# Decode attention on one core: the V loads of 62 units move from SyncE's queue to GpSimd's own

## The chip, the core and the metric

The kernel runs on one core of one Trainium2 chip. The metric is the device time of one execution in microseconds (us); the lower the better. All inputs lie in the chip's memory (HBM), and the output is written back there.

## What is computed

Two blocks, A and B, of the same sizes and with their own inputs: single-token decode attention for 2 sequences, 32 heads of 192 dimensions, a cache of 8192 positions, all in bf16. Their outputs stand side by side.

```
q = (x @ wq)                           # x: 2 x 1 x 640, wq: 640 x 6144
scores = q . k_cache * 192**-0.5       # per head; k_cache: 2 x 32 x 8192 x 192
p = softmax(scores)
o = p . v_cache                        # v_cache: 2 x 32 x 8192 x 192
block = o @ wo                         # wo: 6144 x 640
result = concatenate([A, B], axis=-1)
```

Each number of the caches is used once, so the work is mostly a matter of reading some 837 MB.

## The kernel before

**Units.** A unit is one pair of heads of one sequence of one block; there are 64 of them (u = 0 to 63, `LASTU` = 63). A unit's K is 128 partitions of 49,152 bytes (head and position block on the partitions, 128 positions of 192 dimensions in a partition), and its V has the same shape. Each of the two is fetched by one DMA.

**Buffers.** The tile `big` holds `NBUF` = 3 buffers of that size and two small product buffers. Loads take the buffers in turn in the order of the list `loads`: K(0), K(1), V(0), K(2), V(1), K(3) and so on to K(63), V(62), V(63). Load number i may start when load i-3, which used the same buffer, has been consumed (`done`): for a K that is the fourth multiply of that unit, for a V the end of the weighted sum ("PV"). So K(u) waits for PV of unit u-3, and V(u) waits for the last multiply of K(u). The first V, V(0), waits instead for the last of the projections q, because its buffer holds the weights wq until then; K(1) waits likewise for the projections of block A.

**Work of a unit.** DVE multiplies K by q in four pieces (line 285, `dve_mul`); PE sums the products over groups of dimensions by matmuls with an identity (line 362, `pe_sum`); DVE finishes the sums (line 289) and takes the maximum over positions (line 295); GpSimd takes the maximum over partitions (line 266, `pool_ar`), and ACT makes the bias and the exponentials (lines 315 and 324). PE then forms the weighted sum over V in 64 matmuls (line 376, `pe_pv`), and it does so for unit u after the identity sums of unit u+1. DVE and ACT normalise.

**Order.** Each engine's instructions are put into a table by slot and order (`put`), sorted, and emitted as one stream (`_Stream`), with waits on counting semaphores. DVE, ACT and PE run most units in loops; SyncE (SP) and GpSimd (POOL) are written out. GpSimd's stream is some memsets at the start and then one `pool_ar` per unit.

**Transfers.** All DMAs are issued by SyncE, in one queue, in the order of `loads`: first the weights wq and x, then the K and V, then the pieces of wo, which go into buffers that have become free, and at the end the two outputs. Every DMA is issued at line 245 (`dma`). An issue waits on SyncE until its buffer is free, and what stands behind it waits too. A load adds 16 to the semaphore of its buffer (`bsem`), and its readers wait for the count that belongs to it.

**The end.** The last K and V (units 62 and 63) are followed by the pieces of wo, which take the place of K(63), V(62) and V(63) in the three buffers; PE turns the attention output, multiplies it by wo, and two small DMAs write the result.

Of the kernel before, what the change touches and what calls it, by code (L numbers as in the profile page):

```python
# [117 lines left out]
def build_kernel(nc, blocks, out):  # L118
# [16 lines left out]
    LASTU = NU - 1  # L135
    scale = float(Dh) ** -0.5
    NBUF = 3
# [9 lines left out]
    with ExitStack() as es:  # L147
        sb = lambda name, shape, dt: es.enter_context(nc.sbuf_tensor(name, shape, dt))
        ps = lambda name, shape, dt: es.enter_context(nc.psum_tensor(name, shape, dt))
        sem = lambda name: es.enter_context(nc.semaphore(name))  # L150
# [42 lines left out]
        reg = {}  # L193
        S_sp = _Stream("sp", sem("s_sp"), reg)
# [1 line left out]
        S_act = _Stream("act", sem("s_act"), reg)  # L196
        S_dve = _Stream("dve", sem("s_dve"), reg)
        S_pool = _Stream("pool", sem("s_pool"), reg)
        bsem = [sem(f"bsem{i}") for i in range(NBUF)]

        def dsem(k, n=1):
            reg[k] = (sem("d_" + "_".join(str(i) for i in k)), 16 * n)
# [6 lines left out]
        loads = [("k", 0)]  # L209
# [1 line left out]
            loads += [("k", u), ("v", u - 1)]  # L211
        loads += [("v", LASTU)]
        buf = {}
        bcount = [0] * NBUF
        for i, (kind, u) in enumerate(loads):
            buf[kind, u] = i % NBUF
            bcount[i % NBUF] += 1
            reg[(kind, u)] = (bsem[i % NBUF], 16 * bcount[i % NBUF])

        bk, b62, b63 = buf["k", LASTU], buf["v", LASTU - 1], buf["v", LASTU]  # L220
        assert (bk, b62, b63) == (2, 0, 1)
# [2 lines left out]
        for blk, rows, off, w in ((0, (WR,), woA, [("s", LASTU, NCH - 1)]), (1, (29,), wo0, [("pv", LASTU - 1)]),  # L224
                                  (1, (11, 5, 2, 1), wo1, [("pv", LASTU)])):
            r = 29 if off == wo1 else 0
            for n in rows:
                pieces.append((blk, r, r + n, off, w))
                off, r, w = off + n * D, r + n, []
# [9 lines left out]
        def back(name, u, c, n):  # L239
            i = u * NCH + c - n  # L240
            return (name, i // NCH, i % NCH) if i >= 0 else None

        def dma(out_ap, in_ap, k):
            s = reg[k][0]
            return lambda eng: eng.dma_start(out_ap, in_ap).then_inc(s, 16)
# [13 lines left out]
        def ld_kv(kind, u):  # L259
            hp, b = u // B, u % B  # L260
            blk, h = hp // PPB, 2 * (hp % PPB)
            src = blocks[blk][kind][b, h:h + 2].rearrange("s (p t) d -> (s p) t d", p=64)
            return dma(kv[buf[kind, u]], src, (kind, u))
# [154 lines left out]
        def put(eng, slot, order, fn, waits, sig, tag=None):  # L418
            t = tabs[eng].setdefault(slot, [])
            t.append((order, len(t), fn, waits, sig, tag))  # L420
# [14 lines left out]
        for u in range(NU):  # L435
            for c in range(NCH):
                w = [("k", u), ("pq", NP - 1), ("qa", NP - 1), ("qx", NP - 1), back("s", u, c, 2)]
# [32 lines left out]
        for n, p in enumerate(pieces):  # L470
            w = [("wo", n), ("ot", p[0])]
# [8 lines left out]
        def done(i):  # L480
            if i < 0:
                return None
            kind, u = loads[i]
            return ("m", u, NCH - 1) if kind == "k" else ("pv", u)
# [5 lines left out]
        for i, (kind, u) in enumerate(loads):  # L490
            w = [done(i - NBUF)]
            if i in (1, 2):
                w = [("pq", PPB * i - 1)]
            S_sp.add(ld_kv(kind, u), waits=w)
        for n in range(len(pieces)):
            S_sp.add(ld_wo(n), waits=pieces[n][4])
        for blk in range(NBLK):
# [4 lines left out]
        for n in range(1, HP + 1):  # L502
            S_pool.add((lambda n: (lambda eng: eng.memset(tri[0:n, n:n + 1], 1.0)))(n),
                       waits=[("tri0",)] if n == 1 else [], sig=("tri",) if n == HP else None)
# [5 lines left out]
        for n in range(128 // HP):  # L510
# [3 lines left out]
                  waits=[("id1",), ("place0",)], sig=("place",))  # L514
# [50 lines left out]
def bass_concat_heads__gqa_block_cached__mha_block_cached__decode_kernel(  # L565
    nc: bass.Bass,
    A_x: bass.AP,
    A_k_cache: bass.AP,
    A_v_cache: bass.AP,
    A_wq: bass.AP,  # L570
    A_wo: bass.AP,
    B_x: bass.AP,
    B_k_cache: bass.AP,
    B_v_cache: bass.AP,
    B_wq: bass.AP,
    B_wo: bass.AP,
    out: bass.AP,
):
    blocks = [
        dict(x=A_x, k=A_k_cache, v=A_v_cache, wq=A_wq, wo=A_wo),  # L580
        dict(x=B_x, k=B_k_cache, v=B_v_cache, wq=B_wq, wo=B_wo),
    ]
    build_kernel(nc, blocks, out)
# [28 lines left out]
```

## Time and profile before

| | before |
|---|---|
| median of 3 runs | 1937.1 us (1936.89 to 1937.25) |
| span of the profiled execution | 1936.0 us |
| bytes read from HBM | 836.77 MB |
| mean rate over the span | 432 GB/s |
| busy: PE, DVE, ACT, POOL | 80%, 58%, 7%, 1% |
| queue q1 (SyncE's) of the 16 DMA engines | 99.9% |

The profiled execution has no time beside its span on the page; the median of the other runs is 1.1 us above that span. Engines: PE is TensorE's matmuls, PEld its weight loads, DVE VectorE, ACT ScalarE, POOL GpSimd, SP SyncE. A line number is that of the kernel. The page's 40 slices are equal parts of the span, with the busy share in tenths; the DMA line is the mean over the 16 DMA engines. In a timeline a row begins with the start in us from the span's start and the duration in us; an arrow in brackets names what ended the engine's idle time before it. In the list of waits a row gives the engine and line that waited, what for, and the total in us, the count and the longest. In the list of DMA issues the last number is the median time from issue to landing.

### The profile page before, as it was taken

To read this page: it belongs to the slowest core of one execution; us is meant where nothing else is said; L and a number is where in the kernel's file an instruction comes from. 1 tells how busy PE (TensorE), PEld (TensorE's weight loads), DVE (VectorE), ACT (ScalarE), POOL (GpSimd) and SP (SyncE) were. 2 spreads that over 40 slices of the span, in tenths; PEclk is the share of its full clock that TensorE was granted. 3 is DMA by queue.
4 is the path that set the end of the run, shared out by engine and by line. 5 is a ranking of instruction groups with operands and counts; after the bars stand their busy time and mean duration, and the time that the engine had idled before them with its cause. 6 is when DMAs were issued, how large, how long until landed. Compare 5 with 4: busy or idle time off the path is not lost.

```text
span 1936.0 us, 19059 instructions
## 1 busy us (share of the span) xinstructions
PE 1545.0 (80%) x7728; PEld 743.0 (38%) x7729; DVE 1124.0 (58%) x907; ACT 142.3 (7%) x519; POOL 28.4 (1%) x113
## 2 busy tenths in 40 slices
PE   5777878878878878878878878878878878878878
PEld 2333434434434434434434434433433433433434
DVE  4765565565565565565565565565565565565560
ACT  3100000000000000000000000000000000000000
POOL 0000000000000000000000000000000000000000
PEclk9899989988989988989988999999999999999999
DMA  9999999999999999999999999999999999999999
GB/s 419 427 435 436 432 434 438 430 434 437 434 433 434 437 431 435 437 432 433 436 436 431 434 438 429 436 437 432 434 435 436 430 436 438 428 436 437 433 433 391
DMA packets 19610, 836.91 MB, mean 432 GB/s; under 512 B 2184, under 2 KB 2320, under 8 KB 2576
## 3 DMA queue, kind: packets, MB, share of 16 engines
q1 hardware_dynamic: 19600, 836.78, 99.9%
q8 instruction: 6, 0.10, 0.0%
q14 instruction: 4, 0.03, 0.0%
HBM read 836.77 MB, written 0.01 MB: 432 GB/s over the span
## 4 chain that ended last, share of the span: by engine, by line
DMA 49%; PE 31%; DVE 17%; issue 3%; DVEq 0%; SPq 0%; ACT 0%; ACTq 0%
DMA big<-in_B_k_cache_dram 24%; DMA big<-in_A_k_cache_dram 22%; PE ops L376 18%; DVE big L285 15%; PE scps L362 12%; DMA big<-in_B_wq_dram 2%; DVE sc L289 1%; DMA big<-in_B_wo_dram 1%; PE scps L354 0%; PE ops L368 0%; PE outps L354 0%; DVEq L285 0%; DVE qall L275 0%; PE scps L404 0%; PE oTps L390 0%
## 5 line engine op out<-in xcount | busy, mean ns | idle before, releaser
L285 DVE TENSOR_TENSOR big<-big,qall 128x6144 bf16<-128x6144 bf16 x256 | 852.7, 3351 | 490.7 <-DMA big<-in_B_k_cache_dram 260.6
L362 PE MATMUL scps<-big,ident 128*128 128x512 bf16 x3072 | 815.6, 426 | 358.2 <-DVE big L285 355.7
L376 PE MATMUL ops<-big,pb 128*34 128x384 bf16 x4096 | 676.8, 326 | 0.0
L362 PEld LDWEIGHTS scps<-big,ident 128*128 128x128 bf16 x3072 | 314.3, 107 | 852.7 <-DVE big L285 439.2
L376 PEld LDWEIGHTS ops<-big,pb 128*34 128x34 bf16 x4096 | 395.5, 98 | 258.7
L289 DVE TENSOR_REDUCE sc<-scps 128x32 f32<-128x512 f32 x256 | 175.9, 687 | 227.7 <-PE scps L362 227.7
L315 ACT ACTIVATE nb<-mg 64x1 f32<-64x1 f32 x128 | 25.8, 201 | 1707.7 <-POOL mg L266 1706.9
L324 ACT ACTIVATE pb<-sc,nb 64x128 bf16<-64x128 f32 x128 | 55.8, 436 | 7.8
L266 POOL PARTITION_ALL_REDUCE mg<-mp x64 | 25.7, 402 | 1859.1 <-DVE mp L295 1859.1
L295 DVE TENSOR_REDUCE mp<-sc 64x1 f32<-64x128 f32 x128 | 35.9, 280 | 8.3
L309 ACT ACTIVATE qall<-o_sum,rc 2x192 f32 (+1 forms) x64 | 29.0, 453 | 20.7 <-DVE o_sum L306 19.1
L306 DVE TENSOR_TENSOR o_sum<-ops,o_hi 2x192 f32<-2x192 f32 x64 | 22.1, 346 | 7.7
L354 PE MATMUL scps<-big,xw 128*128 x120 | 23.2, 351 | 2.6 <-DVE xw L271 2.2
L324 ACT ACTIVATION_READ_ACCUMULATOR pb<-sc,nb 64x1 f32 x128 | 23.7, 185 | 0.0
L303 DVE COPY o_hi<-ops 2x192 f32<-2x192 f32 x64 | 22.3, 349 | 2.0
L300 DVE RECIPROCAL rc<-ops 2x1 f32<-2x1 f32 x64 | 10.0, 156 | 21.3 <-PE ops L376 19.3
L275 DVE CAST qall<-scps 64x192 f32 x48 | 17.0, 355 | 7.2 <-PE scps L354 5.4
L280 ACT ACTIVATE qall<-scps 64x192 f32 x48 | 15.6, 324 | 30.5 <-DVE qall L275 28.2
L345 PE MATMUL oTps<-ident,xw 4*128 4x4 bf16 x5 | 0.4, 178 | 21.5 <-DMA xw<-in_B_x_dram 21.5
L354 PEld LDWEIGHTS scps<-big,xw 128*128 128x128 bf16 x120 | 12.4, 103 | 12.1 <-issue 5.9
L368 PEld LDWEIGHTS ops<-ones,rs 128*2 128x2 f32 x128 | 5.5, 82 | 26.9 <-issue 26.9
L404 PE MATMUL outps<-big,oT 128*2 128x320 bf16 x96 | 9.2, 369 | 4.6 <-DMA big<-in_A_wo_dram 4.6
(36 smaller groups left out, 67.6 us busy)
## 6 DMA issues: line engine op xcount, KB each, us to landing
big<-in_A_k_cache_dram SPq DMA_DIRECT2D x32, 6144.0 KB, 28.6
big<-in_A_v_cache_dram SPq DMA_DIRECT2D x32, 6144.0 KB, 27.6
big<-in_B_k_cache_dram SPq DMA_DIRECT2D x32, 6144.0 KB, 28.9
big<-in_B_v_cache_dram SPq DMA_DIRECT2D x32, 6144.0 KB, 27.8
big<-in_A_wq_dram SPq DMA_DIRECT2D x1, 7680.0 KB, 21.2
big<-in_B_wq_dram SPq DMA_DIRECT2D x1, 7680.0 KB, 38.2
big<-in_A_wo_dram SPq DMA_DIRECT2D x1, 7680.0 KB, 29.0
big<-in_B_wo_dram SPq DMA_DIRECT2D x1, 4640.0 KB, 29.3
```

What stands on the lines that cost most here:

```text
L266: return lambda eng: eng.partition_all_reduce(mg[u % 3][:], mp[u % 3][:], 128, bass.bass_isa.ReduceOp.max)
L285: return lambda eng: eng.tensor_tensor(prod[c % 2], t[:, c * TC:(c + 1) * TC, :], qall[:, S_dve.at(u), :].broadcast_to([128, TC, Dh]), ALU ...
L289: return lambda eng: eng.tensor_reduce(sc[u % 3][:, c * TC:(c + 1) * TC], scps[(u * NCH + c) % 3][:], AXL.X, ALU.add)
L295: ins = eng.tensor_reduce(mp[u % 3][r, s:s + 1], sc[u % 3][r, :], AXL.X, ALU.max)
L303: return lambda eng: eng.tensor_copy(o_hi[:], ops[u % 3][32:34, Dh:QW])
L306: return lambda eng: eng.tensor_tensor(o_sum[:], ops[u % 3][0:2, 0:Dh], o_hi[:], ALU.add)
L309: return lambda eng: eng.activation(qall[0:2, S_act.at(u), :], o_sum[:].unsqueeze(1), ACTF.Identity, scale=rc[u % 3][:])
L315: ins = eng.activation(nb[u % 3][r, :], mg[u % 3][r, s:s + 1], ACTF.Identity, scale=-scale)
L324: ins = eng.activation(dst, sc[u % 3][r, :].rearrange("p (g j a) -> p g a j", j=JB, a=2), ACTF.Exp, bias=nb[u % 3][r, :], scale=scale, acc ...
L354: ins = eng.matmul(qps[hp % NQ][:, 0:QW], xbc[:, blk, c, :], wq_t[blk][:, c, S_pe.at(off, QW, QW)], start=(c == 0), stop=(c == DC - 1))
L362: ins = eng.matmul(scps[(u * NCH + c) % 3][:], ident[:], prod[c % 2][:, :, j * DG:(j + 1) * DG], start=(j == 0), stop=(j == NJ - 1))
L376: ins = eng.matmul(ops[u % 3][0:MP, 0:QW], pb[u % 3][:, j0s:j0s + MP], vv[:, j, :], start=(j == 0), stop=(j == TJ - 1))
```

## The change

The loads of V for units 0 to 61 are issued by GpSimd, on a queue of its own. K, the weights, V(62) and V(63) stay on SyncE's queue. A new function `queue` tells the two apart. Since a buffer is now filled from two queues, there is a semaphore for each buffer and queue, with its own count. In GpSimd's stream the load of V(u) stands in slot u ahead of `pool_ar(u)`; it waits there, as it did on SyncE, for the last multiply of K(u). The branch for K in the last part of the diff is never taken with this `queue`.

```diff
-        bsem = [sem(f"bsem{i}") for i in range(NBUF)]
+        bsem = [[sem(f"bsem{i}_{n}") for i in range(NBUF)] for n in range(2)]
...
-        bcount = [0] * NBUF
+        bcount = [[0] * NBUF for _ in range(2)]
+
+        def queue(i):
+            kind, u = loads[i]
+            return 0 if kind == "k" or u > LASTU - 2 else 1
+
         for i, (kind, u) in enumerate(loads):
+            q = queue(i)
             buf[kind, u] = i % NBUF
-            bcount[i % NBUF] += 1
-            reg[(kind, u)] = (bsem[i % NBUF], 16 * bcount[i % NBUF])
+            bcount[q][i % NBUF] += 1
+            reg[(kind, u)] = (bsem[q][i % NBUF], 16 * bcount[q][i % NBUF])
...
             w = [done(i - NBUF)]
             if i in (1, 2):
                 w = [("pq", PPB * i - 1)]
-            S_sp.add(ld_kv(kind, u), waits=w)
+            if queue(i) == 0:
+                S_sp.add(ld_kv(kind, u), waits=w)
+            elif kind == "k":
+                put("pool", u - 2, 3, ld_kv(kind, u), w, None)
+            else:
+                put("pool", u, -1, ld_kv(kind, u), w, None)
```

## The prediction

> **What bounds the kernel now.** I read the page first: engine shares, the 40 slices, the queues, the issues.
>
> ```profile
> PE 1545.0 (80%) x7728; PEld 743.0 (38%) x7729; DVE 1124.0 (58%) x907; ACT 142.3 (7%) x519; POOL 28.4 (1%) x113
> ...
> DMA  9999999999999999999999999999999999999999
> GB/s 419 427 435 436 432 434 438 430 434 437 434 433 434 437 431 435 437 432 433 436 436 431 434 438 429 436 437 432 434 435 436 430 436 438 428 436 437 433 433 391
> ...
> q1 hardware_dynamic: 19600, 836.78, 99.9%
> ...
> big<-in_A_k_cache_dram SPq DMA_DIRECT2D x32, 6144.0 KB, 28.6
> big<-in_A_v_cache_dram SPq DMA_DIRECT2D x32, 6144.0 KB, 27.6
> ...
> big<-in_A_wq_dram SPq DMA_DIRECT2D x1, 7680.0 KB, 21.2
> ```
>
> The busiest compute engine is PE at 80%, but the transfers of SyncE's one queue (q1) fill 99.9% of the time of the 16 DMA engines, in every slice. The bytes are the same after the change, so the time is the wire's time for 836.8 MB, plus whatever stretch the wire is left without work. Next, the windows: is the rate the same in a steady unit as in the mean?
>
> ```profile
> 900.00:929.00 29.00, 23.64 (x112) 11.12 (x111) 17.15 (x13) 1.85 (x7) 0.35 (x1) 0.88 1.00 434
> 1000.00:1029.00 29.00, 23.19 (x114) 11.11 (x114) 17.17 (x14) 1.85 (x7) 0.35 (x1) 0.94 1.00 434
> ```
>
> Columns: stretch, length, busy time of PE, PEld, DVE, ACT and POOL, granted clock, DMA share, GB/s. DMA share is 1.00 at 434 GB/s. A unit needs one K and one V, so a steady unit is 29.0 us of pure transfer, 14.5 us for a load. Then the waits and the timeline of one unit, which tell how far the queue runs ahead.
>
> ```profile
> SPq L245 <- DVE big L285: 958.6, 63, 17.9
> SPq L245 <- PE ops L376: 824.3, 63, 13.1
> ...
> DVE big L285 <- DMA big<-in_B_k_cache_dram: 260.6, 32, 8.4
> DVE big L285 <- DMA big<-in_A_k_cache_dram: 229.1, 30, 9.7
> ```
>
> ```profile
> 911.00 6.63 DVE L285 TENSOR_TENSOR big<-big,qall 128x6144 bf16<-128x6144 bf16 x2 [7.96 <-DMA big<-in_A_k_cache_dram]
> 911.23 0.33 SPq L245 DMA_DIRECT2D big<-in_A_k_cache_dram  x1
> ...
> 927.60 0.33 SPq L245 DMA_DIRECT2D big<-in_A_v_cache_dram  x1
> ...
> 931.91 0.35 POOL L266 PARTITION_ALL_REDUCE mg<-mp  x1 [29.47 <-DVE mp L295]
> ...
> 940.03 6.63 DVE L285 TENSOR_TENSOR big<-big,qall 128x6144 bf16<-128x6144 bf16 x2 [7.17 <-DMA big<-in_A_k_cache_dram]
> 941.05 0.33 SPq L245 DMA_DIRECT2D big<-in_B_k_cache_dram  x1
> ...
> 958.62 1.64 PE L376 MATMUL ops<-big,pb 128*34 128x384 bf16 x9
> ```
>
> Take 911.00, when K(u) is in, as zero. K(u+1) is issued at +0.2 (PV of u-2 has freed its buffer), V(u) at +16.6 (the last multiply of K(u)), the next K is in at +29.0, and PV of u starts at +47.6. Each load lands some 28 us after its issue though it needs 14.5 us of wire: it stands behind one whole load. SyncE's waits are thus waits for a free buffer, and they starve nothing.
>
> **The change, part by part.** Bytes, row length (49,152 bytes; 128 rows over 16 engines, so 8 rows per load and engine) and buffers stay. Moved: the 62 issues of V(0) to V(61), from SP's queue to POOL's. Their 62 x 0.33 = 20 us of SP time (the row at 927.60) were spent on an engine that otherwise waits; gain 0. SP's K no longer stands behind the wait of a V: that wait ended at 927.60 and the next K's own at 941.05, so nothing is let go earlier; gain 0. The semaphores per queue change what is counted, not when; 0. POOL now waits for the last multiply of a unit with the max of L266 queued behind it, but L266 waits anyway for the reduction after that multiply, until 931.91, 4.3 us after 927.60, and what it feeds is not needed before 958.62. Cover: 4.3 us before L266 is late at all, some 25 us before PV is; cost 0.
>
> What is new is that K and V lie in two queues. In one queue, loads are served one after the other; no row shows how two are shared, so this is the unknown. I take it that each DMA engine alternates row by row. Issue to first byte I bound from below by the issue itself, 0.33 us, and from above by the first load: 21.2 us to landing for 7680 KB, whose wire time is 14.5 x 7680/6144 = 18.1, leaves 3.1. I take 1.5, between them, for both queues: neither bound is nearer to a moving queue.
>
> Steady state: K goes on the wire at +1.7, V at +18.1. If K has *a* left at +18.1, sharing ends it at 18.1 + 2a = 29.0, a = 5.45. V then has 14.5 - 5.45 = 9.05 left, and 7.35 when the next K starts 1.7 us later; those share for 14.7 us, V is in at +45.4, K has 7.35 + 1.7 done at the next V's start and 5.45 left again. The cycle closes: when K's queue is empty V has 7.35 us left, when V's is empty K has at least 5.45, and V is in 2.2 us ahead of PV at +47.6. K is in at +29.0 as before. Loss 0, as long as rows keep their speed. Here the new cover ends: it was a whole load (14.5 us), it is now 5.45 and 7.35 us.
>
> The start is the place without this cover:
>
> ```profile
> 1.81 38.17 DMA big<-in_B_wq_dram
> ```
>
> ```profile
> 53.74 0.33 SPq L245 DMA_DIRECT2D big<-in_A_v_cache_dram  x1
> ...
> 72.44 3.35 DVE L285 TENSOR_TENSOR big<-big,qall 128x6144 bf16<-128x6144 bf16 x1
> ...
> 77.18 3.42 POOL L266 PARTITION_ALL_REDUCE mg<-mp  x1 [73.94 <-DVE mp L295]
> ...
> 89.39 0.33 SPq L245 DMA_DIRECT2D big<-in_A_v_cache_dram  x1
> ...
> 98.96 6.63 DVE L285 TENSOR_TENSOR big<-big,qall 128x6144 bf16<-128x6144 bf16 x2 [5.43 <-DMA big<-in_A_k_cache_dram]
> ```
>
> The weights are in at 39.98, K(0) at 54.5, and K(1), V(0), K(2) follow back to back; K(2) is in at 98.9. The first multiply of K(1) runs early, at 72.44, and its last releases V(1) at 89.39, 16.95 later. With two queues V(0) joins at 53.74 + 1.5 = 55.2, within K(1)'s first row. A row takes 14.5/8 = 1.81 us; K(1)'s eighth is then turn 15: 54.5 + 27.2 = 81.7. The multiply slides from 72.44 to about 81.8, V(1)'s issue to 98.75, its first byte to 100.25. K(2), behind K(1), still ends at 98.9, and K(3) must wait for PV(0), which runs only after unit 1's sums. So the wire is bare from 98.9 to 100.25: 1.4 us, call it 1.5. From below 0 (V(0) late by a few us lets K(1) through), from above 4.7 (K(1) ends in turn 16, at 83.5, and an issue takes 3.1: 83.5 + 17.0 + 3.1 - 98.9).
>
> A rule of the trace against the change stands at 77.18: L266 takes 3.42 us beside a multiply of L285 and 0.35 at 931.91 beside none. If POOL's issue of a V is held likewise, that is 3.1 us. In a steady unit it is issued at +16.6, and the next multiply is at +29.0, so nothing holds it; even 3.1 us are less than the 5.45 that K has left. Cost 0 either way; at the start, V(0) at 53.74 is just ahead of the multiplies, and being held shortens the bare stretch.
>
> [...]
>
> The end: the last B_wo load lands 23.45 us after its issue, behind other loads. V(62) and V(63) are on SP in their old order, so the wire's last 23 us keep their work; 0.
>
> ```profile
> 1909.27 23.45 DMA big<-in_B_wo_dram
> ```
>
> Sum: the profiled execution spans 1936.0; + 1.5 = 1937.5. The median of the runs, 1937.1, is 1.1 above that span, so 1938.6 on the scale of the medians; with the bounds 0 and 4.7, 1937.1 to 1941.8. The measurement can tell about 0.2%, 3.9 us, from no change; this is inside it.
>
> **The rivals.**
> *Two busy queues slow the wire.* Turns between two streams, or loads issued into an empty queue, could cost something per row. For: today a queue always has its next load waiting and never wakes from empty, and after the change both do so once a unit. Against: no row. Price: the slices between the first two and the last lie from 428 to 438; if alternating held every slice at the lowest, 1936.0 x 434/428 is +27 us, half of that +13.5: 1952 with the 1.5 of the start, 1941 to 1966.
>
> *They speed it up.* The second stream could fill what lies between rows of the first. For: slices of 438. Against: 99.9% busy and a flat 434 in the windows. Half the way from 434 to the best slice is 436.0/434, -9 us: with the start, 1929.7; the bound 1920.
>
> *V keeps the wire for its whole load once it has the turn* (slower, the mechanism that decides on the other side). Then V goes through in 14.5 us and K waits. Behind two V loads in a row, a delayed K(u) and K(u+1) come back to back: K(u) is in, K(u+1) takes the wire for 14.5, but V(u) is issued 16.6 after the first multiply (0.4 after landing) and is on the wire 1.5 later: 18.5 - 14.5 = 4.0 us bare, less some 0.4 of receipt, 3.6. Two K and two V per such round, 31 rounds: 112 us, 2049. It decides as soon as a turn of the V queue is several rows long; at one row a turn the cover above holds. For: nothing in the trace shows the length of POOL's turns. Against: equal rows in both.
>
> The Trainium skill, "DMA: Bandwidth & Descriptors", section "Queues, rings and completion order", says that an engine takes turns between queues by packets and that a packet is typically 9 to 17 descriptors. By that rule a V of 8 rows and its completion would be one turn, and the time the 2049 of this rival; no run here shows yet whether this page's turn or a single row holds.
>
> *The change does nothing*: the two queues are served in order of issue. Then 1937.1; it lies inside the forecast.
>
> **How the numbers follow.** Forecast 0.50, of which 0.05 is a start that costs over 3.9 us; slower wire 0.24; whole-load turns 0.15 (a rule without a row); faster wire 0.11. Slower: 0.05 + 0.24 + 0.15 = 0.44; same 0.45; faster 0.11. The likeliest case has the range 1937.1 to 1941.8. The range for 8 in 10 reaches past the value of the faster wire towards its bound, and takes in the bounds of the slower wire: 1926 to 1968. It leaves out whole-load turns and a few hundredths at either side.
>
> **What would show it.** Right: a POOL queue of its own with about 62/134 of the loads; DMA 9 in all slices but a gap of 1 to 2 us near 98 to 101 in the start; the first multiply of K(1) near 82 rather than 72.44; K and V each 27 to 29 us from issue to landing; DVE waiting for K as now, 434 GB/s in the windows. Slower wire: DMA share still 1.00 in the windows, with GB/s below 432. Whole-load turns: V landing some 16 us after issue, DMA share under 0.97 in the steady windows. Faster wire: windows above 435. The forecast is wrong if the steady windows are not full, or full at another rate.

## The result and the profile after

| | before | after |
|---|---|---|
| median | 1937.17 us (1936.87 to 1937.41) | 1942.23 us (1940.78 to 1943.04) |
| ratio | | 1.0025, 95% interval 1.0015 to 1.0035 |
| profiled execution: its time, its span | span 1936.0 | 1942.52, span 1941.0 |

Slower by 5.1 us, a quarter of a per cent. The page of the kernel after: the slices, the queues and the issues with the median time to landing.

```profile
GB/s 420 422 404 436 429 433 435 436 432 434 435 435 433 434 436 433 435 431 438 433 435 433 435 436 432 433 435 437 433 432 434 438 434 432 434 436 436 431 433 389
...
q1 hardware_dynamic: 10672, 446.71, 53.2%
q0 software_dynamic: 8928, 390.07, 46.5%
...
big<-in_A_k_cache_dram SPq DMA_DIRECT2D x32, 6144.0 KB, 28.0
big<-in_A_v_cache_dram POOLq DMA_DIRECT2D x32, 6144.0 KB, 29.4
```

One slice stands out: the third (97 to 146 us) moves 404 GB/s where before it moved 435. The windows of before and then of after, for the start and for the steady part (columns as in the prediction: the last two are DMA share and GB/s):

```profile
85.00:110.00 25.00, 22.05 (x116) 10.85 (x117) 17.26 (x12) 1.40 (x6) 0.35 (x1) 1.00 1.00 431
...
300.00:1800.00 1500.00, 1210.85 (x5887) 577.73 (x5886) 890.46 (x671) 94.45 (x357) 18.06 (x51) 0.93 1.00 434
```

```profile
85.00:110.00 25.00, 21.37 (x103) 10.18 (x104) 20.63 (x14) 2.80 (x12) 7.49 (x3) 0.90 0.86 357
...
300.00:1800.00 1500.00, 1171.29 (x5898) 569.26 (x5896) 885.79 (x672) 96.29 (x364) 45.86 (x103) 0.92 1.00 434
```

For 1500 us of steady units the rate on the wire (the 16 DMA engines together) does not differ. In the 25 us around the start's end 74 of 431 GB/s are missing: 74 x 25/434 = 4.3 of the 5.1 us. The share of 0.86 says that for 3.5 us of it, in the mean over the engines, the wire is bare, that is, no row moves; the other 0.8 are rows that took longer. The timeline of the kernel after at that place:

```profile
54.03 0.68 POOL L251 DMA_DIRECT2D big<-in_A_v_cache_dram  x1 [50.78 <-PE outps L360]
...
81.44 3.36 DVE L291 TENSOR_TENSOR big<-big,qall 128x6144 bf16<-128x6144 bf16 x1 [9.46 <-DMA big<-in_A_k_cache_dram]
...
98.87 0.57 POOL L251 DMA_DIRECT2D big<-in_A_v_cache_dram  x1 [9.24 <-DVE big L291]
```

(Line 251 is the DMA issue, 291 the multiply, 272 GpSimd's maximum in this kernel's numbers.) K(1), which shared the wire with V(0), lets DVE begin at 81.44 where it began at 72.44 before; V(1) is issued at 98.87. On the 16 DMA engines K(2) completed between 97.0 and 99.5 us; in the trace's records of single rows V(1)'s first rows began between 100.2 and 101.3 and took 1.9 to 3.3 us each (others 1.8).

### The profile page after: what moved, and what is told of

Same layout as the page of the kernel before. It is cut to its first block, busy times and chain, and to the rows that moved or that the text cites. A ratio compares the mean times of both kernels' runs of the same rounds, so it can differ in the third digit from the quotient of the medians.

```text
span 1941.0 us, 18999 instructions
## 1 busy us (share of the span) xinstructions
PE 1497.7 (77%) x7728; PEld 731.4 (38%) x7729; DVE 1123.9 (58%) x907; ACT 142.4 (7%) x519; POOL 65.1 (3%) x175
## 4 chain that ended last, share of the span: by engine, by line
DMA 49%; PE 32%; DVE 16%; issue 3%; DVEq 0%; SPq 0%
DMA big<-in_A_k_cache_dram 24%; DMA big<-in_B_k_cache_dram 23%; PE ops L382 18%; DVE big L291 14%; PE scps L368 13%; DVE sc L295 1%; DMA big<-in_B_wo_dram 1%; DMA xw<-in_B_x_dram 1%; PE scps L360 1%; PE ops L374 0%; PE outps L360 0%; DVEq L291 0%; PE scps L410 0%; PE oTps L396 0%; DVE xw L277 0%
## 5 line engine op out<-in xcount | busy, mean ns | idle before, releaser
L368 PE MATMUL scps<-big,ident 128*128 128x512 bf16 x3072 | 770.4, 408 | 409.6 <-DVE big L291 397.8
L368 PEld LDWEIGHTS scps<-big,ident 128*128 128x128 bf16 x3072 | 302.9, 104 | 868.6 <-DVE big L291 471.2
L251 POOL DMA_DIRECT2D big<-in_A_v_cache_dram x32 | 17.7, 552 | 795.0 <-DVE big L291 744.2
L251 POOL DMA_DIRECT2D big<-in_B_v_cache_dram x30 | 16.4, 547 | 738.2 <-DVE big L291 738.2
```

Of the source, the lines that this page charges most:

```text
L368: ins = eng.matmul(scps[(u * NCH + c) % 3][:], ident[:], prod[c % 2][:, :, j * DG:(j + 1) * DG], start=(j == 0), stop=(j == NJ - 1))
```

## The experiments

Two theories were set against each other. The *start theory*: the loss is the bare stretch near 98 to 101 us, because V(0) shares the wire with K(1). The *toll theory*: each V load on a second queue costs about 0.08 us, 62 times.

**1. V(0) alone back on SP's queue.**

```diff
-            return 0 if kind == "k" or u > LASTU - 2 else 1
+            return 0 if kind == "k" or u > LASTU - 2 or u == 0 else 1
```

> V(0) alone goes back to SP's queue, behind K(1); V(1) to V(61) stay on POOL's. Start theory (the loss is the stretch near 98 to 101 us in which the wire is bare, because V(0) shares it with K(1)): the first multiply of K(1) is at 72.4 us again, the stretch is gone, and the time is 1937.2 to 1938.5. Toll theory (each of the V loads on a second queue costs some 0.08 us): 61 of 62 tolls stay, 1942.1.

Measured: 1938.01 us, ratio to before 1.0003 (0.9994 to 1.0012): the difference from before is not resolved. DVE begins K(1) at 72.55, and the window of the start is full:

```profile
72.55 3.35 DVE L291 TENSOR_TENSOR big<-big,qall 128x6144 bf16<-128x6144 bf16 x1
```

```profile
85.00:110.00 25.00, 17.91 (x95) 9.10 (x96) 11.49 (x9) 1.40 (x6) 1.05 (x2) 0.90 1.01 435
```

One of 62 moves carries 4.2 of the 5.1 us. The toll theory falls.

**2. V(0) stays on POOL's queue, but comes later.**

```diff
             if i in (1, 2):
                 w = [("pq", PPB * i - 1)]
+            if i == 2:
+                w = w + [("m", 0, 1)]
```

> V(0) stays on POOL's queue, but waits in addition for the second multiply of unit 0 (62.2 us instead of 53.7). Start theory: K(1) has five of its eight rows in before V(0) joins, lands near 71, the first multiply of K(1) is at 72.4 to 73, the bare stretch is gone: 1937.2 to 1938.5. Toll theory: all 62 tolls stay, 1942.2.

Measured: 1938.05 us, ratio 1.0005 (0.9996 to 1.0014), with all 62 loads on POOL's queue.

```profile
62.72 0.68 POOL L251 DMA_DIRECT2D big<-in_A_v_cache_dram  x1 [59.47 <-DVE big L291]
...
74.05 3.36 DVE L291 TENSOR_TENSOR big<-big,qall 128x6144 bf16<-128x6144 bf16 x1 [1.41 <-DMA big<-in_A_k_cache_dram]
...
92.14 0.57 POOL L251 DMA_DIRECT2D big<-in_A_v_cache_dram  x1 [9.91 <-DVE big L291]
```

V(0)'s issue 9 us later brings V(1)'s issue from 98.87 to 92.14, ahead of the end of K(2). What cost was when V(0) joined, not which queue it is on. K(1) came later than I expected, near 74 instead of 71, and its multiply at 74.05 instead of 72.4 to 73, without effect on the time.

**3. The V loads on ACT's queue.**

```diff
-                put("pool", u, -1, ld_kv(kind, u), w, None)
+                put("act", u, -1, ld_kv(kind, u), w, None)
...
-                S_act.emit(eng, [(PQ0, PQ0 + NP, NQ), (3, NSLOT, 3)])
+                S_act.emit(eng, [(PQ0, PQ0 + NP, NQ)])
```

> The same 62 V loads are issued by ACT instead of POOL (ACT's units are then written out instead of looped). Start theory: two queues share the wire as before, K(1) lands near 81 us and the stretch stays with about 3 us: 1941 to 1942.5. If it is POOL's way of issuing that costs: rows at one speed on both queues, and 1937.5 to 1939.

Measured: 1941.52 us, ratio 1.0022 (1.0013 to 1.0031), and the same hole:

```profile
81.31 3.36 DVE L291 TENSOR_TENSOR big<-big,qall 128x6144 bf16<-128x6144 bf16 x1 [9.80 <-DMA big<-in_A_k_cache_dram]
```

```profile
85.00:110.00 25.00, 21.49 (x106) 10.41 (x107) 20.50 (x14) 2.81 (x12) 6.93 (x2) 0.92 0.91 378
```

It is not GpSimd's way of issuing. The hole is smaller (378 instead of 357 GB/s), and the interval overlaps with that of the change, so what ACT's queue saves against POOL's is not resolved.

**4. Nearly all loads on POOL's queue, in one order.**

```diff
-            return 0 if kind == "k" or u > LASTU - 2 else 1
+            return 0 if i == 0 or (kind == "v" and u > LASTU - 2) else 1
```

> K(1) to K(63) go to POOL's queue too, in the order of the list of loads; only the weights, K(0), V(62) and V(63) stay on SP's. One queue serves nearly all loads in turn. Start theory: no sharing, K(1) is in at 69.6 us, no bare stretch, 1937.2 to 1938.5. If POOL's way of issuing costs per load, twice as many loads pay it: 1946 to 1947.

Measured: 1952.78 us, ratio 1.0078 (1.0065 to 1.0092): both expectations missed. Its windows, at the start, in the steady part and near the end:

```profile
78.00:98.00 20.00, 13.66 (x54) 5.28 (x54) 18.76 (x13) 1.40 (x6) 3.84 (x2) 0.91 0.48 187
300.00:1800.00 1500.00, 1159.65 (x5904) 563.29 (x5904) 881.69 (x672) 96.28 (x364) 74.31 (x156) 0.97 1.00 434
1900.00:1916.00 16.00, 13.44 (x73) 6.59 (x71) 9.71 (x10) 1.85 (x7) 0.36 (x1) 1.00 0.75 307
```

```profile
67.08 6.63 DVE L291 TENSOR_TENSOR big<-big,qall 128x6144 bf16<-128x6144 bf16 x2 [12.43 <-DMA big<-in_A_k_cache_dram]
...
88.76 3.42 POOL L272 PARTITION_ALL_REDUCE mg<-mp  x1 [34.13 <-DVE mp L301]
92.05 0.55 POOL L251 DMA_DIRECT2D big<-in_A_k_cache_dram  x1
```

A queue fed by GpSimd alone loses nothing in 1500 us, so there is no toll per load. I had overlooked the two places where two queues still meet: K(0) on SP with K(1) on POOL (DVE begins at 67.08 instead of 55.6), and K(63) with V(62) and V(63). And K(2)'s issue, whose buffer was free when unit 0's multiplies ended (at 87.35, since they began 11.5 us late), now stood behind the maximum of line 272 as well, until 92.05. The wire was about half bare for 20 us at the start and a quarter bare for 16 us at the end: some 10.4 + 4 = 14 of the 15.5 us.

**5 to 8. The length of a turn.** The cover of the steady part rested on one row of each queue per turn. A shorter row on one side shifts the shares, if turns go by rows. Both halves (or quarters) of a load are DMAs of their own. The cut below shows the form that the four edits share; the semaphore counts, and the function that issues the parts in turn, are left out:

```diff
-            return dma(kv[buf[kind, u]], src, (kind, u))
+            parts = [dma(kv[buf[kind, u]][:, n * T // N:(n + 1) * T // N, :], src[:, n * T // N:(n + 1) * T // N, :], (kind, u))
+                     for n in range(N)]   # N = 2 or 4 for the kind that is split
```

> The kernel after, but each V load of POOL's and SP's queue is issued as two DMAs, one for each half of the positions, so that its rows are 24,576 bytes; K's rows stay 49,152. Turn theory (an engine changes queue after every row, whatever its length): beside K(1)'s 8 rows go 8 half rows of V(0), K(1) is in at 54.5 + 8 x 1.81 + 7 x 0.91 = 75.4 us instead of 81.4, V(1) is issued near 93, before the wire runs out at 97 to 99, and the bare stretch is gone; the extra rows add little: 1937.5 to 1942. Equal-share theory (the queues share by time or bytes): K(1) near 81 us, the stretch of 3 us stays, 1942 to 1946.

Measured: 1960.2 us (1946.8 to 1966.9), ratio 1.0106 (1.0077 to 1.0136).

```profile
75.78 3.36 DVE L300 TENSOR_TENSOR big<-big,qall 128x6144 bf16<-128x6144 bf16 x1 [4.04 <-DMA big<-in_A_k_cache_dram]
```

```profile
85.00:110.00 25.00, 19.91 (x96) 9.60 (x95) 16.30 (x10) 1.85 (x8) 1.43 (x3) 0.91 1.00 425
300.00:1800.00 1500.00, 1160.94 (x5826) 565.09 (x5826) 873.96 (x665) 94.29 (x357) 73.45 (x155) 0.93 1.00 429
```

K(1) is in at 75.8 against 75.4 forecast by turns of one row. That is its last engine; the other 15 completed at 73.5 to 74.1, where in the kernel after they stood at 77.1 to 79.6, most of them some 5.4 us later, which is six half rows of 0.91 us. So equal shares by time or bytes fall. The hole of the start is closed in this window; only stretches of up to 1.1 us on single engines are left near 112. The time was missed by both theories: the steady part now runs at 429 GB/s. In the records of single rows there are short bare stretches some 58 to 60 us apart or a multiple of that, 8 us in all, and K's rows take 1.837 us in the mean instead of 1.815, together 11 us per engine, the long ones just behind those stretches.

> The kernel after, but each K load is two DMAs of half the positions, so K's rows are 24,576 bytes and V's stay 49,152. Turn theory: V takes two thirds of the shared wire, V(0) is in first and K(1) last, near 83; the start's stretch grows to 5 us, and in the steady part K is late now and then by about half a microsecond of bare wire every second or third unit: 1950 to 1957. Equal-share theory: as the kernel after with a little more per row, 1942 to 1947.

Measured: 2013.86 us, ratio 1.0397 (1.0374 to 1.0421): the direction of the turn theory, but four to six times the loss that it had worked out (1950 to 1957 expected). The stretch at the start grew to between 4 and 6.7 us over the engines, near the 5 expected; what was far too small was the loss in the steady part, whose window below has 416 GB/s.

> The kernel after, with each K load in four DMAs of a quarter of the positions: K's rows are 12,288 bytes, V's 49,152. Turn theory: V takes four fifths of the shared wire, which is close to the rival of whole-load turns; K is late, two K follow each other, and some 4 us of bare wire stand in every second unit, 31 times: 2060 to 2085, with V landing 17 to 19 us after issue and a DMA share of 0.93 to 0.95 in the steady windows. Equal-share theory: 1942 plus the price of the extra rows, which the next run gives by itself, some 1950 to 1956.

Measured: 2115.26 us, ratio 1.0923 (1.0905 to 1.0942): 30 us above the upper end of the turn theory's 2060 to 2085, with V landing some 21 us after issue instead of 17 to 19. The DMA share of 0.94 is the expected one.

> The kernel before, all loads on SP's queue, with each K load in four DMAs of a quarter of the positions. It gives the price of shorter rows without any sharing. Both theories: no bare wire; 64 x 24 further rows and 64 x 3 further completions per engine at some 7 to 9 ns: 1945 to 1952.

Measured: 1946.00 us, ratio 1.0046 (1.0029 to 1.0062). The steady windows of the half-row and the quarter-row K, and of the quarter-row K on one queue:

```profile
300.00:1800.00 1500.00, 1117.20 (x5632) 542.94 (x5630) 847.73 (x647) 91.32 (x345) 44.50 (x100) 0.91 0.98 416
```

```profile
300.00:1800.00 1500.00, 1067.29 (x5411) 520.87 (x5408) 804.99 (x612) 88.86 (x335) 41.84 (x94) 0.89 0.94 397
```

```profile
300.00:1800.00 1500.00, 1183.05 (x5859) 568.64 (x5856) 883.80 (x667) 94.44 (x357) 18.06 (x51) 0.94 1.01 432
```

Quarter rows by themselves cost 9 us; beside a second queue of long rows they cost 178. POOL's rows in the quarter-row kernel show the cycle that the prediction's third rival described, in which two K follow each other and V cannot be issued yet:

```profile
486.35 0.55 POOL L251 DMA_DIRECT2D big<-in_A_v_cache_dram  x1 [35.57 <-DVE big L300]
...
510.35 0.55 POOL L251 DMA_DIRECT2D big<-in_A_v_cache_dram  x1 [19.61 <-DVE big L300]
...
550.48 0.55 POOL L251 DMA_DIRECT2D big<-in_A_v_cache_dram  x1 [35.73 <-DVE big L300]
```

V issues stand 24.0 and 40.1 us apart: 64.1 for two units, where the wire needs 58.0; the rival had worked out 61.6. The row records have a bare stretch of about 4 us in each such round, with slow first rows after it. So the cycle of that rival exists here, with turns of one row and not of a whole load: it is the ratio of the row lengths that calls it up. Equal-share theory falls here too.

**9. POOL's issue beside a multiply.** V(0) waits for the first reduction, `("r", 0, 0)`, in place of `("m", 0, 1)` of experiment 2.

> V(0) stays on POOL's queue but waits in addition for the first reduction of unit 0, which ends at 64.2 us, when the third multiply of unit 0 (64.2 to 67.5) has just begun. If a multiply holds POOL's issue as it holds its maximum (3.4 instead of 0.35 us), the issue's row lasts some 3 us, to 67.6 or later, instead of 0.55. If it does not, the row lasts 0.55 to 0.7. Either way V(0) joins after K(1) has six or more rows in, the bare stretch is gone and the time is 1937 to 1939.

```profile
64.95 3.35 DVE L291 TENSOR_TENSOR big<-big,qall 128x6144 bf16<-128x6144 bf16 x1
65.68 0.67 POOL L251 DMA_DIRECT2D big<-in_A_v_cache_dram  x1 [62.44 <-DVE sc L295]
```

Measured: one run of 1938.51 us beside 1937.36 of before; the issue's row takes 0.67 us in the middle of a multiply, no more than the 0.68 of experiment 2 beside none. A multiply does not hold the issue's row as it holds line 272 (3.42). In the row records V(0)'s first rows begin at 67.8, as K(1)'s end, and on 11 of the 16 engines before that multiply ends at 68.30; so what the issue sets off was not held until the multiply's end either. Whether it was slowed is left open.

## Why the prediction was right, and where its size was off

The time lay in the range (1926 to 1968), and the likeliest case is what happened: the steady part costs nothing, the start is bare once. Its size was not: 5.1 us instead of 1.5, and 1942.23 stands 0.4 us above the upper end, 1941.8, that the likeliest case had for itself. It fell into the 0.05 that the forecast gave to a start of over 3.9 us.

- *The wire binds, and bytes decide.* Confirmed: DMA share 1.00 and 434 GB/s for 1500 us, in before and after.
- *Moved issues, waits and semaphores cost 0.* POOL issues a V in 0.55 us, and line 272 is as early as before. The steady rows of the kernel after:

```profile
910.67 0.55 POOL L251 DMA_DIRECT2D big<-in_A_v_cache_dram  x1 [29.61 <-DVE big L291]
914.73 0.35 POOL L272 PARTITION_ALL_REDUCE mg<-mp  x1 [3.51 <-DVE mp L301]
934.68 0.55 POOL L251 DMA_DIRECT2D big<-in_A_v_cache_dram  x1 [19.60 <-DVE big L291]
```

- *Queues alternate row by row.* The row records of the kernel after show it: once V(0) has joined, one row of V follows one row of K. K(1)'s multiply was forecast for 81.8 and came at 81.44, but that these agree within 0.4 us is luck, for three differences cancel. V(0)'s first rows came at 58.6 to 59.7 and not at 55.2: three rows of K(1) were ahead of them instead of one, two turns fewer, so that on most engines K(1)'s eighth row ended near 77. Its completion, a record of 4 bytes, then stood behind one more row of V (78.5 to 79.3 on 14 engines). And one engine completed only at 81.0; on one, a 16 KB row of the instruction queue had taken 0.96 us at 66.9 (the records do not name the engines, so that it was the same one is likely and not shown). The forecast for half rows (75.4, came 75.8) has the same three differences; what bears out the rule there is the difference of six half rows.
- *The cover.* The steady cycle is not the one that I worked out: units do not repeat every 29 us but alternate (the idle times before POOL's two issues, 29.61 and 19.60, differ by 10 us). The wire stayed full all the same, so the loss of 0 holds, but the 5.45 and 7.35 us of cover belong to a cycle that did not occur. Experiments 5 and 6, in which half rows on one side leave bare stretches, show that the cover has a limit.
- *The start: the term that was mis-sized.* V(1)'s issue was forecast for 98.75 (98.87), its first byte 1.5 us later (1.3 to 2.4 over the engines). For V(0), beside a busy queue, the same 1.5 was 4.6. What went wrong is the length of the bare stretch: I measured it from 98.9, when the last of 16 engines ends K(2). The engines end between 97.0 and 99.5, and each is bare from its own end: 3.5 us by the window instead of 1.4. The slow first rows after the restart, 0.8, were in no term. Together 4.3 us, inside the bound of 4.7, but that bound was made of other things (a turn more for K(1), an issue of 3.1 us). What remains of the 5.1 is 0.8, and experiments 1 and 2, which have no hole, stand 0.7 to 0.8 above before with intervals that reach down to no difference: not settled.
- *Rivals.* Slower or faster wire: neither; 434 stayed 434. Whole-load turns: none; the cycle worked out for them did not come with equal rows, and came with unequal ones from turns of one row. The rule of "DMA: Bandwidth & Descriptors" in the Trainium skill (turns of a packet, typically 9 to 17 descriptors; section "Queues, rings and completion order") would have given that rival's 2049, an estimate; the row records here show turns of one row of 49,152 or 24,576 bytes.
- *POOL's issue beside a multiply.* V's issue waits for a unit's last multiply, and in the rows above it starts when that ends, so the cost of 0 holds; experiment 9, in the middle of a multiply, did not find the issue's row stretched either.

No version was faster than before. With V(0) held back (experiment 2) no difference from before is resolved.

## What to carry to other kernels

When the transfers are the bound, ask of any second queue only one thing: does the wire ever run out of issued work? Two queues hand the wire out row by row, so the load that is needed first no longer comes first, and the place where that bites is where few loads are in flight, at the start and at the end; here one wait that let the urgent load pass first repaired it. Keep rows of equal length in queues that share the wire, and count a bare stretch for each DMA engine from its own end, plus a slow restart.

## What the runs showed of the hardware

- Two queues take turns by rows, not by bytes or time: K(1) was in at 81.4 us beside equal rows and at 75.8 beside half rows, and the row records alternate. A load's completion takes a turn too: K(1)'s came behind one more row of V on 14 of 16 engines.
- From the issue of a V to its first row it took 1.3 us into a bare wire (98.87 to 100.15) and 4.6 beside a busy queue (54.03 to 58.6).
- The first rows on all 16 engines after a bare stretch take 1.9 to 3.3 us instead of 1.8, some 0.8 us per restart. In the kernel with quarter rows the first rows behind the bare stretches at 483 and 547 us took 1.9 to 3.6 us.
- A row of 12,288 bytes takes 0.460 us and one of 49,152 takes 1.815, so a row costs under 10 ns of its own: 24 more rows per K load and engine, 64 times, came to 9 us.
- Loads issued by SP, ACT and GpSimd run at the same 434 GB/s.
